# Fewer filling matmuls, range tests moved to the end, more word buffers and a new hand-written order in a fused linear-attention and gated-MLP kernel

## Chip, cores and metric

One core of a Trainium2 chip runs the whole program. The metric is the device time of one execution in microseconds (us), given as the median of some runs. A profile is one more execution, taken by the hardware profiler. Engines are named as the profile names them: PE (TensorE), DVE (VectorE), ACT (ScalarE), POOL (GpSimd), SP (SyncE, here a DMA queue).

## What is computed

The reference is a complex linear recurrence for 4 x 8 heads over 768 steps with 48 x 48 states, followed by a two-layer MLP over all 3072 tokens. In short:

```
a = (a_re + i a_im) * min(|a|, 0.999) / (|a| + 1e-6)      # per head, step, channel d
S_t = a_t * S_(t-1) + k_t v_t^T        # complex state, the real part is read
y_t = q_t . Re(S_t)
h = x @ w_in;  g = h * tanh(softplus(h));  out = g @ w_out   # 384 -> 2048 -> 384
```

## The kernel before

**Tiling.** The 3072 tokens are 12 *units* of 256 tokens (4 batches, 3 units each); a unit is two *chunks* a and b of 128. For each unit `elementwise` (L319) turns a_re and a_im into growth factors and phases: squares, logarithms, exponentials, arctan, sine and cosine on ACT, products, scans and roundings on DVE; q and k are multiplied by them and sent through DMAs ("relays", L534) into the row layout `T`. Units 0 and 1 (`SUMMED`) take their running sums by matmuls against triangular constants `turn` and `less` (`sum_up`, L381) in place of DVE scans. `attention` (L556) does a chunk as matmuls: transposes of k (`kn`), the causal 128 x 128 products (`am`), the output (`y`), the state (`pd`, `hold`). DMAs (`x move`, L675) lay y out as the MLP's input `x`. `moe` (L698) then runs 8 column blocks: first product `mm1` (L720), gate chain exp, cap, square, ln, inv on ACT and DVE, `gate` (L733), second product `mm2` (L757). Unit 0 is "plain": fp32 operands (192 first-product and 64 second-product matmuls, half a unit at a time, blocks `q0` to `q3` for halves a and b). Units 1 to 11 use three fp32r products of high and low parts (`xH`, `xL`, `wh`, `wl`; blocks `p0` to `p7`).

**Weights.** `weight(i)` (L256) loads one of 16 weight tiles as 64-bit words in a two-buffer pool (`words`, L263) and rebuilds it bit by bit: `low` (ACT or DVE), `shift`, `join` (DVE, L274, L278), `carry` (POOL or DVE, L282). `halves(i)` (L290) later makes `wh` (`high`, L298) and `wl` (`rest`, L303).

**Order.** Every step is registered as an operation with a list of engines allowed; the literal `ORDER` (L52) gives the sequence in which all operations are issued and, by a letter, an engine other than the first allowed one. Each engine executes its own operations in that sequence and waits where one is not ready; so do the DMA queues of SP and ACT. A position below is the index in that sequence. Buffers are taken in the same sequence.

**Filling.** 69 `spin` operations (L816, `SPINS`, L41) of two bf16 matmuls of 512 columns each, "junk", stand between PE's other operations from the start up to the second products of unit 0's half b; their PSUM tile has the tag `po`, two buffers, which the second products use too (L814).

**Range test.** For all units a `test` (L456) on DVE counts the elements with a_re - 0.55 >= a quarter of a_im squared into `good`; at the end `verdict` (L820) sums these counts, and a general path runs if one fails.

Of the kernel before, what the change touches and what calls it, by code (L numbers as in the profile page):

```python
# [55 lines left out]
146 202 149 231 72 148 71 206 204 108 234 236 151 150 68 154 237 73 207 200 156 208 600 152 240 109 157 465 155 181
160 238 601 175 161 203 239 182 209 602 183 176 177 184 178 110 153 245 185 179 241 393 217 394 180 467 111 242 218
187 186 389 219 243 189 220 188 244 192 205 392 190 390 463 193 391 191 250 195 246 196 221 247 305 222A 396 223 224A
599 194 400 398 469 306 399 248 401A 402 210 197 307 249 397 604 403 316 213 212 211 255 471 308 408A 608 409 606 309
315 407 251 777 252 310 419 214 317 253 112 325 311 318 420 254 312 256 113 215 319 313 609 320 260 114 611 610 115  # L60
216 421 257 321 423 605 473 314 258 422 404 424 425 259V 430 261 262 427 265 411 405 336 475 426 413 406 263 414 412A
428 415 607 264 431 322 417A 416 616 433 429 776 434 418 266 335 784 267 270 617 477 326 268 781 432 116 269 612 117
327 436 118 119 120 782 275 345 479 328 613 121 329 122 271 123 124 337 272 125 615 435 273 126 614 127 338 128 274
276 277 129 130 339 131 783 132 133 340 134 280 627A 437 481V 135 341 278 136 330 438 440 618 395 619 279 331 137 332
323 342 439V 324 281 282 285 483 410 283 442 598 626A 620 597 346 284 441 443 356 621 347 485 290 355 286 348 287 333
623 628 288 357 464 334 622 289 358 447 450 343 624 966 349 295 625 365 291 359 344 350 292 629 448 360 445 293 351
630 444 361 635 352 294 296 362 632 451 446 636 634 353 487 453 489 454 354 456 455 297 363 637 449 298 639 364 461
457V 638 452 299 459 462 300 375 631 640 780 491 366 458 642 460 466 965 376 641 367 786 633 301 368 496 302 369 468
643 377 495 370 303 644 645 470 371 304 647 646 372 788 649 778 378 779 507 497 508 648 650 651 785 379 652 970 472
380 373 787 973 474 381 374 789 498 382 499 654 476 385 520 509 655 386 478 500 383 790 510 480 501 656 791 792 519  # L70
482 653 493 657 384 484 511 971 793 659 512 658 661 387 502 513 388 660 521 532 662 972 522 663 503A 514 523 794 664
515A 524 531 969 665 504 796 667 516 544 533 668 797 795 505 666 534 525 798 669 806 807G 506 535 672 536 543 526 670
808G 537 673 517 674 799 545 555 675 538 527 556 800 528 518 557 546 539 547 558 529 540 548 801 559 530 549 486 560
541 550 803 542 488 492 567 804 810 568 551A 805 579 552 569 813 817 811 553 816 580 561 814 570 671 818 571 562 554
820 572 494 676 822 581 563 573 812 582 677 564 583 819 574 584 815 565 490 575A 823 585 802 689 821 576 678 1157 586
# [967 lines left out]
```

## Time and profile before

| | |
|---|---|
| median of 3 runs | 615.82 us (615.81 to 618.37) |
| the profiled execution | 614.4 us |
| its span, first to last instruction | 612.7 us |
| PE, DVE, ACT busy | 596.7, 465.5, 496.8 us |
| instructions | 12061 |

The profiled execution is 1.7 us longer than its span and 1.4 us shorter than the median. Busy time is the union of an engine's instructions; a busy PE includes the junk.

### The profile page before, as it was taken

How to read it: one execution, taken by the hardware profiler on the slowest of the kernel's cores; microseconds unless marked ns; L12 is line 12 of the kernel's file. 1: busy time of each engine (PE TensorE's matmuls, PEld its weight loads, DVE VectorE, ACT ScalarE, POOL GpSimd, SP SyncE). 2: the span in 40 equal slices, each digit the busy share in tenths (PEclk: the TensorE clock that was granted, in tenths of full speed). 3: DMA queues.
4: the chain of work that ended last, by engine and by line, in shares of the span. 5: the costliest groups of instructions: out<-in, count | busy, mean ns of one | idle time of the engine just before them, and what ended most of it. 6: DMA issues, size and time to landing. Idle time of an engine off the chain costs nothing.

```text
span 612.7 us, 12061 instructions
## 1 busy us (share of the span) xinstructions
PE 596.7 (97%) x4712; PEld 555.4 (91%) x4712; DVE 465.5 (76%) x806; ACT 496.8 (81%) x790; POOL 48.8 (8%) x45
## 2 busy tenths in 40 slices
PE   8999999899999999999999999999999999999995
PEld 4688777889899999999999999999999999999995
DVE  5999788899889979996969969848967455455352
ACT  8899877798899999999989999868995615659381
POOL 1122343101000110000000001000011000000000
PEclk9999999999999999999999999999999999999999
DMA  8777765711516354135234153115144030020000
GB/s 287 225 231 212 233 197 166 207 54 28 173 57 169 92 154 132 43 103 168 79 116 118 53 152 89 46 50 133 53 130 105 22 84 1 2 53 2 28 1 30
DMA packets 56673, 65.51 MB, mean 107 GB/s; under 512 B 4768, under 2 KB 50208, under 8 KB 56608
## 3 DMA queue, kind: packets, MB, share of 16 engines
q1 hardware_dynamic: 55952, 64.16, 36.1%
q8 instruction: 39, 0.64, 0.4%
q10 hardware_dynamic: 656, 0.49, 0.3%
q14 instruction: 26, 0.21, 0.1%
HBM read 36.18 MB, written 4.72 MB: 67 GB/s over the span
## 4 chain that ended last, share of the span: by engine, by line
PE 49%; ACT 28%; DVE 9%; DMA 5%; issue 4%; SPq 3%; POOL 0%; ACTq 0%; DVEq 0%; POOLq 0%
PE po L757 17%; PE ph L720 17%; ACT e L170 11%; ACT X L170 6%; ACT L168 5%; PE junk L818 5%; PE pa L594 4%; PE ypsum L612 3%; SPq L534 2%; PE pd L625 2%; DMA T<-X 1%; ACT R L170 1%; DVE g L733 1%; DMA x<-y 1%; DVE gl L745 1%
## 5 line engine op out<-in xcount | busy, mean ns | idle before, releaser
L720 PE MATMUL ph<-xH,wh 128*128 128x256 f32 x462 | 133.1, 288 | 1.9 <-DVE g L733 1.8
L720 PE MATMUL ph<-xL,wh 128*128 128x256 f32 x462 | 129.8, 281 | 0.0
L720 PE MATMUL ph<-xH,wl 128*128 128x256 f32 x462 | 129.7, 281 | 0.0
L170 ACT ACTIVATE e<-e 128x512 f32<-128x512 f32 x192 | 117.2, 626 | 11.2 <-DVE e L789 10.3
L757 PE MATMUL po<-wh,gh 128*128 128x384 f32 x308 | 106.4, 346 | 0.0
L757 PE MATMUL po<-wh,gl 128*128 128x384 f32 x308 | 104.4, 339 | 0.0
L757 PE MATMUL po<-wl,gh 128*128 128x384 f32 x308 | 104.1, 338 | 0.0
L720 PEld LDWEIGHTS ph<-xH,wh 128*128 128x128 f32 x462 | 87.0, 188 | 4.5 <-DVE g L733 2.3
L733 DVE SCALAR_TENSOR_TENSOR g<-e,ph 128x512 f32<-128x512 f32 x96 | 65.3, 683 | 31.4 <-ACT e L170 28.4
L720 PEld LDWEIGHTS ph<-xL,wh 128*128 128x128 f32 x462 | 87.0, 188 | 0.1
L720 PEld LDWEIGHTS ph<-xH,wl 128*128 128x128 f32 x462 | 87.0, 188 | 0.0
L168 ACT ACT_TABLE_LOAD x58 | 74.4, 1283 | 1.4 <-issue 0.4
L789 DVE TENSOR_SCALAR e<-e 128x512 f32<-128x512 f32 x96 | 46.3, 485 | 35.6 <-ACT e L170 35.0
L170 ACT ACTIVATE e<-ph 128x512 f32<-128x512 f32 x96 | 56.6, 592 | 17.4 <-PE ph L720 14.6
L745 DVE TENSOR_TENSOR gl<-g,gh 128x512 fp32r<-128x512 f32 x88 | 61.6, 703 | 10.7 <-PE po L757 7.2
L170 ACT ACTIVATE e<-e,fifth 128x512 f32<-128x512 f32 x96 | 68.5, 720 | 1.0
L757 PEld LDWEIGHTS po<-wh,gh 128*128 128x128 f32 x308 | 57.9, 188 | 0.7 <-issue 0.7
L757 PEld LDWEIGHTS po<-wh,gl 128*128 128x128 f32 x308 | 57.9, 188 | 0.3 <-DVE gl L745 0.2
L757 PEld LDWEIGHTS po<-wl,gh 128*128 128x128 f32 x308 | 57.8, 188 | 0.0
L594 PE MATMUL pa<-T 96*128 96x128 f32 x384 | 48.8, 277 | 0.6 <-DVE S L636 0.4
L594 PEld LDWEIGHTS pa<-T 96*128 96x128 f32 x384 | 46.2, 191 | 2.3 <-DVE S L636 0.6
L601 DVE TENSOR_TENSOR am<-pa,cmask 128x512 f32<-128x512 f32 x48 | 32.3, 686 | 7.7 <-PE pa L594 7.3
(128 smaller groups left out, 1094.1 us busy)
## 6 DMA issues: line engine op xcount, KB each, us to landing
T<-X SPq DMA_DIRECT2D x71, 129.0 KB, 2.5
T<-QK SPq DMA_DIRECT2D x70, 129.0 KB, 2.5
words<-w_in SPq DMA_DIRECT2D x8, 768.0 KB, 4.6
words<-w_out SPq DMA_DIRECT2D x8, 768.0 KB, 5.2
QK<-k SPq DMA_DIRECT2D x12, 384.0 KB, 4.5
QK<-q SPq DMA_DIRECT2D x12, 384.0 KB, 4.5
V<-v SPq DMA_DIRECT2D x12, 384.0 KB, 3.8
out_dram<-o SPq DMA_DIRECT2D x24, 192.0 KB, 1.9
```

The source lines that it names most:

```text
L168: self.nc.scalar.preload_act_table_set(need)
L170: return self.nc.scalar.activation(out, in_, func, **kw)
L534: e.dma_start(to[part * NJ + j], st[src][:, c, j])
L594: e.matmul(d["pa", g][:, i, :], T()[:, 4 * g + i, 1, :C], T()[:, 4 * g + i, 0, :C], start=True, stop=True)
L601: e.tensor_tensor(d["am", g], d["pa", g], cmask.unsqueeze(1).broadcast_to([P, 4, C]), ALU.mult)
L612: e.matmul(ypsum[64 * par:64 * par + D, i, :], lhs, rhs, start=m == 0, stop=first or m == 1)
L720: e.matmul(ph[k][:, slot(k, j, a), :], win(x, j, kt, a), st[y][:, kt, cols(k)], start=n == 0, stop=n + 1 == len(todo))
L733: e.scalar_tensor_tensor(g_[k], e_[k], 2.5, ph[k], ALU.subtract, ALU.mult)
L745: e.tensor_tensor(gs[k][1], g_[k], gs[k][0].bitcast(F32), ALU.subtract)
L757: e.matmul(po[t], x[:, slot(k, j, a), 0 if halved else t * P:C if halved else (t + 1) * P], wout(y, j, a), start=j == 0 and a == 0 and n == 0,
L789: op("V", f"{n} cap", lambda e, k=k: e.tensor_scalar_min(e_[k], e_[k], math.exp(20.0)))
L818: e.matmul(junk["junk"], cmask, cmask.unsqueeze(1).broadcast_to([P, 4, P]), start=True, stop=True)
```

## The change

- `SPINS` goes from 69 to 40.
- Units 0 and 1 lose their four half-unit `test` operations in `steps`; a new function `test(u)` registers, with the verdict at the end, a reload of a_re and a_im, a square (ACT or DVE) and one test for each of the two units.
- Unit 1's clamp of the log magnitude, a DVE `tensor_scalar`, becomes an ACT `Relu` with scale and bias; its magnitude sum uses `less` for both halves.
- Word tiles rotate over six places: the two buffers as before, and four that later hold `wh` pairs (`wp6` to `wp3`).
- The constants are built in another sequence on POOL (`cmask` first, `identity` late); `good` is zeroed.
- `ORDER` is a new list (2434 operations, before 2459). It also chooses other engines for some: up to unit 1's first MLP product, 11 of the carries go to DVE and 3 to POOL (before 2 and 13), 3 of the `low` to DVE (before none), 13 relays and 3 x moves to the ACT queue (before 3 and 2), and 6 `high` come ahead of it on ACT (before 14). Table loads on ACT, which follow from the sequence of functions, are 44 (before 58), 12 of them ahead of that product (before 10).

```
@@ -38,8 +38,10 @@
 SPLIT_UNITS = 2
 PLAIN = (8, 0)
 HALVED = (0,)
-SPINS, SPIN = 69, 2
+SPINS, SPIN = 40, 2
+WORDS = ("words", "words", "wp6", "wp5", "wp4", "wp3")
 SUMMED = 2
+CLIPPED = (1,)
 HELD = 2
 XRUNS = ((0, 0, 0, 32), (0, 1, 32, 16), (64, 1, 64, 16), (0, 2, 80, 32))
 LOW, HIGH, FADED = 0.55, 2e6, 1e-17
@@ -49,103 +51,103 @@
 TABLE = {AF.Exp: EXPLN, AF.Ln: EXPLN, AF.Arctan: TRIG, AF.Sin: TRIG}
 
 ORDER = [(int(x.rstrip("VAGTS")), x.lstrip("0123456789")) for x in """
-74 0 1 75 2 5 76 3 77 159 7 158 78 8 4 10 79 225 9 11 230 25 80 12 6 15 13 162 26 81 595 16 82 596 27 83 18 17 28V 84
-14 30 85 29 19 31 32 20 166 21 38 23 24 86 22 41 87 163 42 88 33 47 89 164 90 43 49 34 48 91 227 165 92 167 35 93 168
...
+72 0 1 73 127 2 74 3 75 128 4 7V 76 8 5 10V 9 77 192 11G 12 197 78 79 24V 13 132V 14 19 27V 80 22 81 82 25 83 15 28 84
+133 17 85 16 135V 31 18 26 32 29 134 86 23 33 87 34 21 166V 88 20 89 42 46 47G 137 35 48 169V 136 30 90 43V 138 45 36
...
@@ -219,9 +221,22 @@
     nc.scalar.preload_act_table_set(EXPLN)
     op.table = EXPLN
 
-    identity = const.tile([P, P], F32, name="identity")
-    make_identity(nc, identity)
-    ident = identity[:2 * D, :2 * D]
+    cmask = const.tile([P, P], BF16, name="cmask")
+    nc.gpsimd.memset(cmask, 1.0)
+    nc.gpsimd.affine_select(
+        out=cmask, in_=cmask, compare_op=ALU.is_ge, fill=0.0, base=0,
+        pattern=[[1, P]], channel_multiplier=-1,
+    )
+    halfpi = const.tile([P, 1], F32, name="halfpi")
+    nc.gpsimd.memset(halfpi, math.pi / 2)
+    tiny = const.tile([P, 1], F32, name="tiny")
+    nc.gpsimd.memset(tiny, 1e-30)
+    fifth = const.tile([P, 1], F32, name="fifth")
+    nc.gpsimd.memset(fifth, 0.2)
+    clip = const.tile([P, 1], F32, name="clip")
+    nc.gpsimd.memset(clip, math.log(0.999))
+    above = const.tile([P, 1], F32, name="above")
+    nc.gpsimd.memset(above, 1.0 / 0.999)
     sums = {}
     for n, x in (("turn", INV2PI), ("less", -2.0 * INV2PI)):
         sums[n] = const.tile([P, P], F32, name=n)
@@ -230,28 +245,20 @@
             out=sums[n], in_=sums[n], compare_op=ALU.is_ge, fill=0.0, base=0,
             pattern=[[1, P]], channel_multiplier=-1,
         )
-    cmask = const.tile([P, P], BF16, name="cmask")
-    nc.gpsimd.memset(cmask, 1.0)
-    nc.gpsimd.affine_select(
-        out=cmask, in_=cmask, compare_op=ALU.is_ge, fill=0.0, base=0,
-        pattern=[[1, P]], channel_multiplier=-1,
-    )
+    identity = const.tile([P, P], F32, name="identity")
+    make_identity(nc, identity)
+    ident = identity[:2 * D, :2 * D]
     rmask = const.tile([P, NJ * NCH, C], U8, name="rmask")
     nc.gpsimd.memset(rmask, 1.0)
     nc.gpsimd.memset(rmask[:, :, 0:1], 0.0)
-    halfpi = const.tile([P, 1], F32, name="halfpi")
-    nc.gpsimd.memset(halfpi, math.pi / 2)
-    tiny = const.tile([P, 1], F32, name="tiny")
-    nc.gpsimd.memset(tiny, 1e-30)
-    fifth = const.tile([P, 1], F32, name="fifth")
-    nc.gpsimd.memset(fifth, 0.2)
     good = const.tile([P, UNITS + SPLIT_UNITS, 3], F32, name="good")
+    nc.gpsimd.memset(good, 0.0)
     ncar = const.tile([P, NJ], F32, name="ncar")
     ypsum = ps.tile([112, 4, C], F32, name="ypsum", bufs=1)
     nc.vector.memset(ypsum[32:64], 0.0)
 
 
-    w, wh, wl, words = {}, {}, {}, {}
+    w, wh, wl, words, pairs = {}, {}, {}, {}, {}
 
     def weight(i):
         src = (w_in, w_out)[i % 2][i // 2]
@@ -260,7 +267,9 @@
             return words[i].bitcast(U32).rearrange("p (n two) -> p n two", two=2)[:, :, n]
 
         def load(e):
-            words[i] = me.tile([P, WC], I64, tag="words", name="words", bufs=2)
+            slot = WORDS[i % len(WORDS)]
+            pool, bufs = (me, 2) if slot == "words" else (wts, 1)
+            words[i] = pool.tile([P, WC], I64, tag=slot, name="words", bufs=bufs)
             e.dma_start(words[i], src)
 
         def low(e):
@@ -290,7 +299,9 @@
     def halves(i):
         def high(e):
             if i < NW - 2:
-                wh[i] = wts.tile([P, WC], F32R, tag=f"w{NW + i}", name="wh")
+                if i // 2 not in pairs:
+                    pairs[i // 2] = wts.tile([P, 2, WC], F32R, tag=f"wp{i // 2}", name="wh")
+                wh[i] = pairs[i // 2][:, i % 2]
                 wl[i] = None
             else:
                 both = me.tile([P, 2, WC], F32R, tag="words", name="whl", bufs=2)
@@ -389,7 +400,7 @@
             def mag(e):
                 pm[0] = bank("mag")
                 for j in range(NJ):
-                    for a, x in enumerate(("turn", "less")):
+                    for a, x in enumerate(("less" if u in CLIPPED else "turn", "less")):
                         e.matmul(pm[0][:, j, :], st["X"][:, c, j, a, :C], sums[x], start=a == 0, stop=a == 1)
 
             def phase(e):
@@ -453,16 +464,23 @@
                 op("AV", f"{n} size i", size_i)
                 op("VG", f"{n} size", lambda e: e.tensor_tensor(half(0), half(0), half(1), ALU.add))
                 op("VG", f"{n} slope", lambda e: e.tensor_tensor(I(), I(), x1(), ALU.mult))
-                op("V", f"{n} test", lambda e: e.scalar_tensor_tensor(
-                    half(1), R(), LOW, half(1), ALU.subtract, ALU.is_ge, accum_out=good[:, gi(g), 0:1]))
+                if not summed:
+                    op("V", f"{n} test", lambda e: e.scalar_tensor_tensor(
+                        half(1), R(), LOW, half(1), ALU.subtract, ALU.is_ge, accum_out=good[:, gi(g), 0:1]))
                 op("A", f"{n} arctan", lambda e: act(I(), I(), AF.Arctan))
                 op("A", f"{n} mag ln", lambda e: act(half(0), half(0), AF.Ln, scale=4.0, bias=tiny))
                 op("A", f"{n} mag exp", lambda e: act(half(1), half(0), AF.Exp, scale=-0.5))
-                op("A", f"{n} mag eps", lambda e: act(half(1), half(1), AF.Ln, scale=1e-6, bias=1.0))
-                op("V", f"{n} mag clamp", lambda e: e.tensor_scalar(
-                    half(0), half(0), 2.0 * math.log(0.999), -1.2, ALU.min, ALU.max))
+                if u in CLIPPED:
+                    op("A", f"{n} mag eps", lambda e: act(half(1), half(1), AF.Ln, scale=1e-6 / 0.999, bias=above))
+                    op("A", f"{n} mag clip", lambda e: act(half(0), half(0), AF.Relu, scale=-0.5, bias=clip))
+                else:
+                    op("A", f"{n} mag eps", lambda e: act(half(1), half(1), AF.Ln, scale=1e-6, bias=1.0))
+                    op("V", f"{n} mag clamp", lambda e: e.tensor_scalar(
+                        half(0), half(0), 2.0 * math.log(0.999), -1.2, ALU.min, ALU.max))
                 if summed:
-                    sum_up(n, g)
+                    for c in (g,) if isinstance(g, int) else range(NCH):
+                        sum_up(n if isinstance(g, int) else f"{n}{'ab'[c]}", c)
+                        yield
                     return
                 op("V", f"{n} mag", lambda e: e.scalar_tensor_tensor(R(), half(0), 0.5, half(1), ALU.mult, ALU.subtract))
                 op("V", f"{n} mag scan", lambda e: e.tensor_tensor_scan(
@@ -545,11 +563,19 @@
 
         for late in (False, True):
             for g in groups:
-                steps(g, late)
-                if summed and not late:
-                    yield
+                yield from steps(g, late)
         if not summed:
             yield
+
+    def test(u):
+
+        st = Tiles({"R": (io, "R", 2, [P, NJ * TU]), "I": (io, "I", 2, [P, NJ * TU])})
+        op("S", f"R{u} again", lambda e: e.dma_start(st["R"], are[u]))
+        op("S", f"I{u} again", lambda e: e.dma_start(st["I"], aim[u]))
+        op("AV", f"u{u} size again", lambda e: act(st["I"], st["I"], AF.Square, scale=0.5) if e is nc.scalar
+           else e.scalar_tensor_tensor(st["I"], st["I"], 0.25, st["I"], ALU.mult, ALU.mult))
+        op("V", f"u{u} test", lambda e: e.scalar_tensor_tensor(
+            st["I"], st["R"], LOW, st["I"], ALU.subtract, ALU.is_ge, accum_out=good[:, u, 0:1]))
 
     state = {}
 
@@ -855,6 +881,8 @@
             for i in range(NW):
                 halves(i)
         if u + 1 == UNITS:
+            for i in range(SUMMED):
+                test(i)
             verdict()
         moe(u, units[u], u * TU)
     with tc.manual_schedule():
```

## Rows read from the trace of the kernel before

**Rows 1.** The page: busy time by engine (us, share of the span, instructions), and its group of DVE's cap (busy us, mean ns of one, idle before).

```profile
PE 596.7 (97%) x4712; PEld 555.4 (91%) x4712; DVE 465.5 (76%) x806; ACT 496.8 (81%) x790; POOL 48.8 (8%) x45
...
L789 DVE TENSOR_SCALAR e<-e 128x512 f32<-128x512 f32 x96 | 46.3, 485 | 35.6 <-ACT e L170 35.0
```

**Rows 2.** Busy time in stretches of the span: from:to, length, then busy us and instruction count of PE, PEld, DVE, ACT, POOL, the granted clock as a share of full speed, DMA share, GB/s.

```profile
0.00:83.00 83.00, 78.79 (x574) 57.20 (x574) 65.97 (x112) 74.11 (x127) 22.46 (x27) 1.00 0.73 228
83.00:110.30 27.30, 27.25 (x184) 21.65 (x185) 24.99 (x36) 18.65 (x28) 8.92 (x5) 1.00 0.69 202
110.30:200.00 89.70, 86.20 (x694) 81.24 (x693) 81.18 (x134) 82.09 (x129) 4.38 (x3) 1.00 0.40 112
200.00:300.00 100.00, 99.08 (x807) 95.74 (x805) 87.98 (x151) 99.44 (x153) 3.77 (x4) 1.00 0.38 108
300.00:600.00 300.00, 298.88 (x2426) 293.43 (x2425) 204.00 (x373) 220.93 (x353) 9.26 (x7) 1.00 0.24 66
```

**Rows 3.** The chain of waits that ended last, followed back from the end: start us, length us, engine and line; the pieces with junk.

```profile
2.57 7.20 PE junk L818 x24
...
13.11 6.04 PE junk L818 x28
...
74.40 6.91 PE junk L818 x32
...
83.05 2.85 PE po L757 x8
```

**Rows 4.** From the timeline: weight loads of the first junk matmuls, PE's first matmul of unit 1's MLP, and DVE's gate for unit 0's half b, block q0 (start us, duration us).

```profile
2.97 0.15 PEld L818 LDWEIGHTS <-cmask 128*128 128x128 bf16 x1 [0.28 <-issue]
3.40 0.15 PEld L818 LDWEIGHTS <-cmask 128*128 128x128 bf16 x1 [0.28 <-issue]
...
6.37 2.90 PEld L818 LDWEIGHTS <-cmask 128*128 128x128 bf16 x14 [0.26 <-issue]
...
64.67 0.68 DVE L733 SCALAR_TENSOR_TENSOR g<-e,ph 128x512 f32<-128x512 f32 x1
...
110.31 0.36 PE L720 MATMUL ph<-xH,wh 128*128 128x256 f32 x1
```

**Rows 5.** DVE in the timeline (a start follows the one before it by less than a duration, since instructions overlap by some 0.09 us): the prices of carry, join, shift, squares, test, clamp.

```profile
17.57 0.57 DVE L274 TENSOR_SCALAR w<-words 128x768 uint32<-128x768 uint32 x1
18.04 0.43 DVE L462 TENSOR_SCALAR X<-X 128x384 f32<-128x384 f32 x1
...
19.24 0.56 DVE L456 SCALAR_TENSOR_TENSOR X<-R,X 128x384 f32<-128x384 f32 x1
...
20.93 0.96 DVE L282 CUSTOM_DVE_ANT_0 w<-words,w 128x1536 uint16<-128x1536 uint16 x1
21.80 0.96 DVE L447 SCALAR_TENSOR_TENSOR X<-I 128x768 f32<-128x768 f32 x1
```

**Rows 6.** POOL's carries and DVE beside them, from the timeline.

```profile
23.61 0.96 DVE L503 TENSOR_TENSOR QK<-QK,X 128x768 f32<-128x768 f32 x1
...
28.58 2.09 DVE L456 SCALAR_TENSOR_TENSOR X<-R,X 128x384 f32<-128x384 f32 x1
...
34.19 2.07 DVE L462 TENSOR_SCALAR X<-X 128x384 f32<-128x384 f32 x1
...
40.06 1.85 POOL L282 TENSOR_TENSOR w<-w,words 128x768 int32<-128x768 int32 x1 [4.08 <-DVE w L278]
...
40.44 2.29 DVE L503 TENSOR_TENSOR QK<-QK,X 128x768 f32<-128x768 f32 x1
```

**Rows 7.** DVE's and ACT's costliest groups in the first 110 us: busy us, mean ns.

```profile
L789 DVE TENSOR_SCALAR e<-e 128x512 f32<-128x512 f32 x7 | 7.0, 999 | 5.2 <-ACT e L170 5.2
...
L479 DVE SCALAR_TENSOR_TENSOR I<-ncar,I 128x3 f32<-128x3 f32 x1 | 1.2, 1224 | 0.0
...
L170 ACT ACTIVATE words<-words 128x768 int32<-128x768 uint32 x15 | 13.8, 923 | 0.9 <-DMA words<-w_out 0.8 <-DMA words<-w_in 0.2
L168 ACT ACT_TABLE_LOAD x10 | 12.8, 1283 | 0.5 <-issue 0.4
L298 ACT CAST wh<-w 128x768 fp32r<-128x768 f32 x13 | 10.6, 824 | 0.9 <-ACT words L170 0.7 <-POOL w L282 0.2
```

**Rows 8.** The ACT queue's DMA issue, and waits of ACT and DVE for a weight tile, from the timeline (in brackets the idle time before and what ended it); last, from the view of DMA issues, the loads of a_re (KB each, median us to landing).

```profile
45.23 0.63 ACTq L534 DMA_DIRECT2D T<-QK  x1
45.90 1.28 ACT L168 ACT_TABLE_LOAD   x1 [0.37 <-issue]
...
112.36 0.56 DVE L274 TENSOR_SCALAR w<-words 128x768 uint32<-128x768 uint32 x1 [2.05 <-DMA words<-w_out]
...
112.36 0.93 ACT L170 ACTIVATE words<-words 128x768 int32<-128x768 uint32 x1 [2.50 <-DMA words<-w_out]
...
R<-a_re SPq DMA_DIRECT2D x10, 384.0 KB, 3.8
```

**Rows 9.** Stretches of 20 us as in rows 2, and the end.

```profile
20.00:40.00 20.00, 19.15 (x155) 14.26 (x155) 18.16 (x33) 17.91 (x34) 3.90 (x2) 1.00 0.82 240
40.00:60.00 20.00, 19.53 (x167) 16.78 (x162) 18.52 (x26) 18.41 (x31) 6.42 (x3) 1.00 0.72 216
...
520.00:540.00 20.00, 20.00 (x146) 19.75 (x146) 9.87 (x18) 10.62 (x19) 0.00 (x0) 1.00 0.00 1
...
609.00:612.70 3.70, 0.00 (x0) 0.00 (x0) 0.00 (x0) 0.49 (x1) 0.00 (x0) 0.70 0.15 55
```

More of the change, by code (lines that the diff above doesn't have):

```diff
@@ L56 @@
[L56 to L75, printed above, removed]
[7 rows of a table removed]
@@ new lines @@
+1558 1556 1250 1718 1251 1270 1559V 1721 1288 1557 1719 1260 1271 1289 1722 1261 1724 1560 1886 1290 1562 1720 1881
+1262 1887 1272 1279 1561V 1394 1280 1273 1281 1291 1263 1725 1292 1282 1274 1293 1283 1730 1393 1294 1284A 2055 1275
+1727 1285 1395 1729 1295 1564 1731 1563 1296A 2054 1405 1882 1552 1723 1396 1286 1297 1565 1287 1406 1298 1407 1397
+1408 1299 1883 1398 1409 1418 1300 1302 1717 1417 1399 1303 1410 1301 1400 1567 1688 1885 1419 1566 2062 1420 1569
+1401 1411 1402 1568 1571 1888 1421 1430 1574 1422 1412 1728 1572 1423 1429 1576 1424 1441 1726 1431 1577 1432 1442
@@ new lines @@
+1488 1598 1599 1608 1489 1906 1600 1609 1590 2069 1743 1908 1491 1490 1741 1744 1909 1591 1740 1492 1610 1900 1601
+1745 2246 1907 1602 1748 1746 1901 1611 1603 1750 1612 1747 1613 1620 1742V 1904 1614 1592 1911 1621 1749 1902 1593
+1632 1903 1751 1622 1604A 1615 2245 1633 1910 2071 1905 1594 1623 1634 1605 1752 2076 1635 1753 1636 1913 1624 1754V
+1915 1625 1595 2077 2072 1758 1626 1755 1637 1645 1757 2250V 1606 1912 2253V 2251 1627 1756 1644 2074 1616 2058 1628
+1638 1617 1656 1646 1763V 2056 1764 2252 1647 1607 2057 1639 1648 2073 1657 1629 1649 1759V 1618 2078 1650 1761 1669
@@ new lines @@
+1793 1935 1936 1803 1794 1804 1937 1785 1795 1774 1805 1941 1940 1786 1806 2103 1938V 1775 1807 1796 1945 2262 1813
+1947 1797 2101 1814 1942 1808 1946 2263 1776 1944 1815 2095 1825 2100 2271 2327 1787 2094 2088 1943 1948 1950V 1788
+1798 1816 2247 1951 1826 1952V 2248 1949 1953 1837 2326 2104V 1827 1809 1817 2105 1810 2265 2107 2106 1799 1818 2108
+2272 2109 2114 2110 2111 2264 1828 2115 2112 2116 1819 2275 1829 2119 1838 2277A 1830 1820 1800 2276 2120V 1839 2117
+1849 1831 1821 2118G 1840 2273 1850 2274 2121 1832 2123 1822 1811 1833A 1851 1812 1954 1841 1852 2279 1842 1823 1843
@@ new lines @@
+2018 1999 2009 2019 2293 2295 2020 1988 2021 1989 2144 2294 2039 2027 2000 2028 2010A 2297 2038 2298 2029 2145 2296V
+2040 2329 2030 2001 2031 2032 2146 2332 2033 2299 2041 2147 2304 2300 2301 2148 2011 2149 2302 2022 2305 2034 2306
+2303 2042 2309 2307 2333 2043 2311 2150 2044 2158 2045 2157 2023 2308 2012 2310 2159 2151 2013 2024 2035 2046A 2025
+2036 2047 2312 2037 2048 2049 2313 2050 2052 2152 2051 2314 2334 2053 2160 2153 2169 2161 2154 2170 2182 2171 2162
+2172 2181 2163 2173 2155 2164 2174 2194 2315 2175 2316 2183 2156 2176 2319 2184 2318 2193 2165 2185 2166 2317 2186
@@ new lines @@
+2205 2177 2320V 2187 2206 2324 2188 2195 2322V 2196 2167 2207 2208 2335 2217 2178 2209 2189 2197 2168 2198 2218 2199
+2210 2200 2179 2211 2323 2190 2219 2180 2212 2220 2191 2321 2221 2222 2192 2201A 2213 2336 2223 2229 2224 2230 2325
+2202 2338 2214 2231 2232 2337 2233 2203 2339 2234 2204 2235 2215 2236 2225 2350 2226 2340 2349 2341 2216 2351 2237A
+2352 2227 2342 2238 2353 2228 2354 2343 2239 2355 2240 2361 2241V 2243V 2242 2362 2344 2244 2345A 2373 2363 2346 2374
+2364 2356 2365 2347 2366 2375 2385 2367 2376 2357 2377 2386 2358 2368 2348 2387 2378 2359 2388 2369 2379 2397 2389
@@ L149 @@
+2380 2370 2398 2409 2399 2390 2360 2391 2371 2392 2400 2410 2401 2402 2421 2381A 2393 2411 2382 2372 2412 2383 2413
+2394 2403 2422 2404 2405 2384 2423 2414 2395 2406 2415 2424 2396 2416 2425 2417 2426 2407 2418 2427 2408 2428 2419
+2429A 2430 2420 2431 2432 2433A
 """.split()]
```

116 lines of the change are left out of this document (64 added, 52 removed), and 26 rows, old and new, of the table ORDER.

## The prediction, made before the changed kernel ran

> **What bounds the kernel now.** Read first where each engine is busy, then the same by stretches, then who waits. Over the whole span TensorE (PE) is busy 596.7 of 612.7 us [rows 1], but that holds the junk. By stretches [rows 2], from 110.3 to 600 us PE stands still for 3.5 + 0.9 + 1.1 = 5.5 us: there it is the bound, and nothing on the other engines pays. Before 83 us it stands still for only 4.2 us too, of which 2.6 before its first instruction, yet this is no real load: the chain shows pieces of junk as long as 7.2, 6.0 and 6.9 us [rows 3]. A warm junk matmul takes 6.91 / 32 = 0.216 us there; the first ones load their weights 0.43 us apart [rows 4]. So 138 of them cost 9 x 0.43 + 129 x 0.216 = 31.7 us of PE's order.
>
> What does real work wait for in this front? ACT is busy 74.1 and DVE 66.0 of 83 us [rows 2]: the two together feed PE, ACT somewhat more. I take as mark M the first matmul of unit 1's MLP, at 110.3 us [rows 4]. What PE has to do before and after M is the same in both orders within one or two blocks. So the question is when M comes; the 502.4 us behind it stay, as PE is the bound there. Up to M real work takes 110.3 - 2.6 (start) - 31.7 (junk) - 1.7 (other waits) = 74.3 us.
>
> **The change, part by part.**
>
> *Fewer spins.* 58 matmuls x 0.216 = 12.5 us leave PE's order. All lie ahead of M. PE's floor for M becomes 110.3 - 12.5 - 1.7 = 96.1 us. It is reached only if operands come that early. One point speaks for it: the gate for half b's first block is done at 64.67 + 0.68 = 65.4 us, but its second product starts at 83.05, behind the last piece of junk [rows 3, 4]; junk holds one of the two `po` buffers until then. In the new order the last spin stands ahead of half b's first product, so the buffer is free long before.
>
> *DVE up to M.* It is busy 66.0 + 25.0 = 91.0 us there [rows 2]. Counted from both orders, with prices start to start [rows 5]: nine more carries x 0.87 = 7.8; three `low`, not seen on DVE before (as `shift`, which reads the same words with the same stride, 0.47; as the carry at most 0.87, which adds 1.2; I take the first) = 1.4; seven half squares x 0.47 and a full one of 0.87 = 4.2; two weight subtractions x 0.87 = 1.7; three evictions = 1.5. That is 16.6 more. Gone: four tests x 0.56 = 2.2, two clamps 0.9, roundings 1.4, a size and a slope 0.9, one join 0.9, a cast and copies 0.7: 7.0. Net +9.6.
>
> *POOL's carries.* Against this stands what a carry on POOL does to DVE. With one running, a product takes 2.29 us instead of 0.96, a test 2.09 instead of 0.56, a clamp 2.07 instead of 0.43 [rows 5, 6]; the seven caps have a mean of 0.999 against 0.485 over the kernel [rows 1, 7]; a link of three elements takes 1.22 [rows 7]. Excess: 1.3 + 1.5 + 1.6 + 3.6 + 1.1 = 9.1 us for 13 carries, 0.7 each; ten fewer give back 7.0. Two half-width operations of units 0 and 1 go to POOL instead: +0.7 by half that price each. The ends are 0 and 9.1. DVE's busy time to M becomes 91.0 + 9.6 - 7.0 + 0.7 = 94.3 us. The Trainium skill (SBUF — State Buffer, "Who interferes with whom") has the loser of the port that DVE and GpSimd share blocked for the whole instruction of the other; by that, ten carries of 1.85 us would give back up to 18.5 us, DVE would fall to 85.8 us, and M to PE's floor. The rows show only 9.1 in all, as many carries fall beside work that needs no second port or wait themselves; I keep 7.0.
>
> *ACT up to M.* Busy 74.1 + 18.7 = 92.8 us [rows 2]. Off: four `low` (0.92 each) 3.7, eight `high` (0.82) 6.6 [rows 7], squares and their readings about 4; on: two more table loads 2.6 [rows 7], clips, roundings and more of the gate chain about 4. It comes to about 85. Eleven more DMA issues go through ACT's queue: one takes 0.63 and left ACT idle for 0.37 [rows 8], so 0 to 6.9 us, at 0.37 each 4.1. ACT ends at 89, under DVE: the bound in front passes from ACT to DVE. What waits behind those issues is ACT's own next activation, and a relay there also waits for DVE's turn product; this belongs to the use of the engines below.
>
> *Word buffers.* The wait for a weight tile just behind M, 2.05 us on DVE and 2.50 on ACT [rows 8], comes from a two-buffer pool; with six places the loads go out earlier. It lets DVE keep its pace up to M; I book nothing apart.
>
> *When M comes.* Between 20 and 60 us DVE was busy 36.7 of 40 us, a share of 0.917 [rows 9], the best long stretch of the front that is not held by PE. I take this share: 94.3 / 0.917 = 102.8 us, 7.5 earlier than 110.3. Between M and PE's floor 6.7 us of waits then stand where junk stood. The ends: the floor of 96.1, and DVE's share over the whole front before, 91.0 / 110.3 = 0.825, which gives 114.3.
>
> *Behind M.* Eight `high` come after M now (6.6 us of ACT); ACT had 7.6 us free up to 200 us and none up to 300 [rows 2], but 16 table loads fewer behind M give it 20.5 us. DVE has 8.5 and 12 free there against some 10 us more work spread to the end. I book nothing; without that cover up to 2 us.
>
> *Tests at the end.* Two squares and two tests of 0.96 us each and four loads of 3.8 us [rows 5, 8], placed where DVE is busy 9.9 of 20 us and DMA idle [rows 9]. SP's queue takes the reloads between unit 11's relays; the third waits for unit 11's last reading of R. Nothing booked; up to 1 us if relays come late. The other start sequence on POOL lets junk begin up to 1 us earlier; nothing, as later waits take it up.
>
> **Sum.** Span 612.7 - 7.5 = 605.2. The profiled execution lies 1.7 us above its span and the median 1.4 above that (615.82 against 614.4): 605.2 + 3.1 = 608.3 us.
>
> **Rivals.**
>
> *The floor.* Junk was pure delay and M comes at 96 to 97: 615.8 - 14.2 = 601.6 us. For it: the second product that stood 17.7 us behind its gate. Against: DVE would need 0.98 of its time.
>
> *Waits take the place of all the junk.* M stays at 110: 616 us, no change. For it: DVE and ACT have together almost the same work, 183.8 before and 183 after, and both were near 0.9 in the first 60 us. Against: ACT was idle for a third of 83 to 110 us [rows 2], so the front as a whole has room.
>
> *Slower: DVE, now the busiest, is used no better than before.* At 0.825 M comes at 114.3, 4 us late: 619.8. It decides where DVE's share to M is under 0.83. For it: in-order waits on ACT, whose queue now holds relays.
>
> *Slower: the clock.* The granted clock is 1.00 in all stretches up to the end, 0.70 in the last 3.7 us, when PE had nothing left to do [rows 2, 9]. At the start junk comes every 0.43 us against 0.216 later, the spacing of 1.2 against 2.4 GHz [rows 3, 4]. Behind the last spin PE has no filler, with up to 17 us of waits to M if DVE is slow. If the clock falls to 1.2 GHz for matmuls worth 10 us, they take 20, half of it hidden in waits: 114.3 + 5, 625 us. The Trainium skill (TensorE: Matmul & The Clock Gate, Part 1) calls the throttled rate the default, which activity releases; by that rule filling less costs. The end of the trace agrees, no wait inside it does (none is that long).
>
> *The new places don't bring the weights sooner,* since loads queue on SP behind relays: the 2 us at M stay, 610.3 us.
>
> **How the numbers follow.** Forecast (M from 98 to 106, 603.5 to 611.5): 0.55. Floor 0.10. Weights late 0.05. No change 0.16. DVE slower 0.08. Clock 0.06. A measurement here tells about 0.5%, 3.1 us, from no change. Faster by more than that: 0.55 + 0.10 + 0.05 = 0.70; same 0.16; slower 0.14. The range 601 to 617 takes in the floor and the case of no change, and leaves out the two slow ones, 0.14.
>
> **What would show it.** Right: 80 junk matmuls, the last before 65 us; M near 103; DVE's busy time to M 92 to 97 us at a share near 0.92, ACT's under it; single carries on DVE of 0.96; PE idle some 5 to 9 us between 20 us and M, on DVE or relays; granted clock 1.00 up to M; the 500 us behind M as before. Wrong: M at 110 or later, idle time of PE behind M well over 6 us, a clock under 1.00 in the front, or PE waiting for unit 11's relays near the reloads.

## The result and the profile of the changed kernel

The changed kernel takes 600.87 us (median of 4 runs, 598.65 to 603.12) against 615.82 for the kernel before (4 runs, 615.72 to 618.37): ratio 0.9748, 95% interval 0.97 to 0.9795. It is faster, as forecast, but by 14.95 us instead of 7.5, and 0.1 us below the lower end of the range. The profiled execution took 601.94 us, its span 600.2. That execution lies 1.1 us above its median, the profiled one of the kernel before 1.4 under its own; so the spans, which the traces explain, differ by 12.5 us and not by 14.95.

The sum of the prediction can be laid beside the trace at two places, the mark M (PE's first matmul of unit 1's MLP) and the last matmul. First the timeline at M, then the last matmul (start us, duration us):

```profile
107.93 0.58 PE L746 MATMUL ph<-xH,wh 128*128 128x256 f32 x1
...
594.36 0.34 PE L783 MATMUL po<-whl,gh 128*128 128x384 f32 x1
```

| us | before | after | forecast | measured |
|---|---|---|---|---|
| start to M | 110.3 | 107.9 | -7.5 | -2.4 |
| M to the end of the last matmul | 496.2 | 486.8 | 0 | -9.4 |
| behind it | 6.2 | 5.5 | 0 | -0.7 |
| span | 612.7 | 600.2 | -7.5 | -12.5 |

So the total came nearer than its parts by luck: the front gave a third of its forecast, the stretch that was booked at nothing gave most of the gain, and the two errors partly cancel. The 9.4 us are firm: in eight further kernels that keep the changed order behind M (runs 2 to 6 and 10 to 12 below) that stretch takes 486.8 to 487.3 us, and 495.9 in the old order of run 1. The 2.4 us are less so: M came at 110.3, 112.4 (run 7) and 112.1 (run 8) in three profiles of the same old front, and at 107.9 and 107.5 (run 9) in two of the new one.

The stretches, to be laid beside [rows 2] (columns as there):

```profile
0.00:83.00 83.00, 71.95 (x520) 56.55 (x521) 65.62 (x123) 60.91 (x101) 10.76 (x26) 0.94 0.73 241
83.00:107.90 24.90, 24.90 (x181) 20.45 (x181) 24.30 (x34) 24.64 (x40) 2.45 (x1) 1.00 0.43 139
107.90:200.00 92.10, 91.66 (x747) 87.68 (x746) 89.20 (x155) 90.77 (x140) 8.84 (x5) 1.00 0.46 133
200.00:300.00 100.00, 100.00 (x837) 98.39 (x836) 89.51 (x158) 85.75 (x136) 1.60 (x1) 1.00 0.36 99
300.00:594.00 294.00, 294.00 (x2373) 290.40 (x2372) 203.47 (x378) 206.32 (x333) 5.23 (x4) 1.00 0.25 71
```

See first that in [rows 2] PE is busy 99.08 of 100 us from 200 to 300, here 100.00, a difference of 0.9 us; but it ran 807 matmuls there and runs 837 here. From M to 300 us it ran 694 + 807 = 1501 in 189.7 us, 126.4 ns each, and now 747 + 837 = 1584 in 192.1, 121.3 ns each. Behind 300 us it is 300 / 2426 = 123.7 and 294 / 2373 = 123.9 ns, the same. So most of the 9.4 us lie between M and 300 us (1501 x 5.1 ns = 7.7, if the mix of matmuls is alike). Now the whole stretch from M to the last matmul, first before, then after, with 3957 and 3956 matmuls:

```profile
110.30:606.50 496.20, 490.65 (x3957) 476.58 (x3955) 374.55 (x659) 403.57 (x635) 17.41 (x14) 1.00 0.29 82
107.90:594.70 486.80, 486.36 (x3956) 476.86 (x3954) 382.18 (x689) 383.02 (x607) 15.67 (x10) 1.00 0.32 89
```

PE's idle time falls from 5.55 us to 0.44, which is 5.1 of the 9.4. The other 4.3 us lie in its busy time, 490.65 against 486.36 for the same work at the same granted clock. They are most likely short waits that the trace counts as busy, since ends of matmuls are modelled; no row shows them one by one.

Then all waits of PE, which is the whole list (us in total, times, longest):

```profile
PE pkn L608 <- DMA T<-QK: 5.8, 2, 5.2
PE pkn L608 <- DMA R<-a_re: 3.4, 1, 3.4
PE junk L844 <- POOL cmask L226: 1.7, 1, 1.7
PE pa L620 <- ACT kn L613: 0.3, 1, 0.3
PE psum L409 <- ACT I L172: 0.2, 1, 0.2
```

All but the 0.3 lie before M. For the second, the trace names the load of `a_re` as what came last; the matmul reads `T`, and a relay to `T`, issued on ACT's queue at 20.96 us, landed 5.8 us later, just before the wait ended. The chain of waits says the same by engine, first the kernel before, then the changed one:

```profile
PE 49%; ACT 28%; DVE 9%; DMA 5%; issue 4%; SPq 3%; POOL 0%; ACTq 0%; DVEq 0%; POOLq 0%
```

```profile
PE 78%; ACT 10%; DMA 5%; DVE 3%; issue 2%; SPq 1%; POOL 0%; DVEq 0%; ACTq 0%; POOLq 0%
```

In the front, the stretches that answer to [rows 9], and from the timeline the two waits with what stands around the second (in brackets the idle time before and what ended it):

```profile
20.00:40.00 20.00, 16.64 (x127) 13.43 (x125) 16.96 (x33) 11.94 (x21) 6.53 (x3) 0.91 0.80 243
40.00:60.00 20.00, 19.39 (x184) 18.16 (x182) 20.00 (x33) 17.64 (x31) 0.28 (x1) 1.00 0.73 245
60.00:80.00 20.00, 14.84 (x110) 12.40 (x109) 12.29 (x25) 11.26 (x19) 0.00 (x0) 0.83 0.85 296
```

```profile
27.05 0.87 PE L608 MATMUL pkn<-identity,T 96*128 96x96 f32 x4 [3.37 <-DMA R<-a_re]
...
66.06 1.46 PE L783 MATMUL po<-w,g 128*128 128x384 f32 x4
...
72.68 1.51 PE L608 MATMUL pkn<-identity,T 96*128 96x96 f32 x8 [5.16 <-DMA T<-QK]
73.98 2.82 PE L783 MATMUL po<-w,g 128*128 128x384 f32 x4
```

The same four matmuls take 1.46 us before the wait of 5.16 and 2.82 behind it: TensorE runs there at the lower of its two clocks, 1.2 in place of 2.4 GHz. The granted clock is 0.50 from 72.7 to 76.5 us, and 0.83 over the stretch. Of the table of M: PE starts 0.9 us earlier, junk takes 9 x 0.43 + 71 x 0.216 = 19.2 us instead of 31.7 (the last piece starts at 51.2), other waits take 11.1 - 1.7 = 9.4 instead of 1.7, and the rest 77.6 instead of 74.3 for as many matmuls (621 and 620): -0.9 - 12.5 + 7.7 + 3.3 = -2.4. The 3.3 more are, by estimate, work at the low clock: behind the two waits PE is busy for some 8.7 us at 0.50, which can cost up to 4.4.

What PE waited for at 72.68 is a relay. The DMA issues of that time:

```profile
61.69 0.53 SPq L370 DMA_DIRECT2D R<-a_re  x1
62.32 0.46 SPq L273 DMA_DIRECT2D words<-w_in  x1
62.83 0.45 SPq L273 DMA_DIRECT2D words<-w_out  x1
63.33 0.42 SPq L273 DMA_DIRECT2D words<-w_in  x1
63.73 0.55 ACTq L552 DMA_DIRECT2D T<-QK  x1
64.62 0.33 SPq L273 DMA_DIRECT2D words<-w_out  x1
```

Within 3 us SP's queue issues a_re (384 KB) and four weight tiles of 768 KB, a burst that the six places allow. The relay of 129 KB that ACT's queue issues among them, at 63.73, lands 8.7 us later. It is the burst and not ACT's queue: a relay that the same queue issued at 61.40, ahead of the burst, landed in 2.8 us, and the same relay in run 4 below, where one load of 768 KB is issued in place of four, in 4.2.

### The profile page after: what moved, and what is told of

Its sections match the earlier page's. It is cut to its first block, busy times and chain, and to the rows that moved or that the text cites. A ratio compares the mean times of both kernels' runs of the same rounds, so it can differ in the third digit from the quotient of the medians.

```text
span 600.2 us, 11935 instructions
## 1 busy us (share of the span) xinstructions
PE 583.2 (97%) x4654; PEld 553.9 (92%) x4654; DVE 472.1 (79%) x844; ACT 469.1 (78%) x747; POOL 28.9 (5%) x37
## 4 chain that ended last, share of the span: by engine, by line
PE 78%; ACT 10%; DMA 5%; DVE 3%; issue 2%; SPq 1%; POOL 0%; DVEq 0%; ACTq 0%; POOLq 0%
PE po L783 30%; PE ph L746 30%; PE pa L620 6%; PE ypsum L638 6%; PE pd L651 4%; ACT e L172 3%; ACT X L172 3%; DMA T<-QK 2%; PE pkn L608 2%; ACT L170 1%; DMA R<-a_re 1%; DMA QK<-k 1%; DMA V<-v 1%; ACT wh L309 1%; ACT gh L765 0%
## 5 line engine op out<-in xcount | busy, mean ns | idle before, releaser
L771 DVE TENSOR_TENSOR gl<-g,gh 128x512 fp32r<-128x512 f32 x88 | 60.9, 694 | 13.6 <-ACT gh L765 7.5
L815 DVE TENSOR_SCALAR e<-e 128x512 f32<-128x512 f32 x96 | 40.3, 421 | 32.0 <-ACT e L172 31.5
L620 PE MATMUL pa<-T 96*128 96x128 f32 x384 | 50.1, 280 | 0.3 <-ACT kn L613 0.3
L620 PEld LDWEIGHTS pa<-T 96*128 96x128 f32 x384 | 47.5, 195 | 1.6 <-ACT kn L613 0.5
L627 DVE TENSOR_TENSOR am<-pa,cmask 128x512 f32<-128x512 f32 x48 | 32.5, 685 | 13.6 <-PE pa L620 13.6
```

The lines of the kernel that those rows point to most:

```text
L620: e.matmul(d["pa", g][:, i, :], T()[:, 4 * g + i, 1, :C], T()[:, 4 * g + i, 0, :C], start=True, stop=True)
L627: e.tensor_tensor(d["am", g], d["pa", g], cmask.unsqueeze(1).broadcast_to([P, 4, C]), ALU.mult)
L771: e.tensor_tensor(gs[k][1], g_[k], gs[k][0].bitcast(F32), ALU.subtract)
L815: op("V", f"{n} cap", lambda e, k=k: e.tensor_scalar_min(e_[k], e_[k], math.exp(20.0)))
```

## The experiments

All ratios are against the kernel before, run on the same chip as the run: medians 616.28 us (runs 1, 4, 5, 8), 615.53 (2, 3, 6, 7) and 615.84 (9 to 12), single executions 613.8 to 620.1. M and what stands behind it come from one profiled execution of each. "Behind M" is the time from M to the end of the last matmul.

**1. The old order with 40 spins.**

```
+    spun = []
     def spin(e):
-        for _ in range(SPIN):
+        spun.append(0)
+        for _ in range(SPIN if len(spun) <= 40 else 0):
```

> The kernel before with its last 29 spins empty (40 left, 80 junk matmuls), its order untouched. T1 (junk was delay): the mark M, PE's first matmul of unit 1's MLP, comes 4 to 9 us earlier than 110.3 and the time is 607 to 612. T2 (waits take the junk's place, DVE and ACT bound the front): M stays within 2 us and the time is 614 to 618. T3 (clock): the granted clock falls under 0.95 in the stretch of 60 to 85 us and the time is over 618.

616.56 us, ratio 1.001 (0.9981 to 1.0039); M at 110.81. Waits stand where junk stood, on ACT (4.53 us), relays and DVE, and the clock falls behind them:

```profile
60.00:80.00 20.00, 12.76 (x111) 11.38 (x109) 14.52 (x22) 16.72 (x26) 7.64 (x3) 0.85 0.56 179
80.00:100.00 20.00, 18.96 (x118) 15.33 (x120) 17.19 (x27) 15.80 (x24) 8.14 (x4) 0.89 0.67 223
```

Up to M PE stands still for 13.6 us, 9.3 more than before, and its work without junk takes 78.0 us instead of 74.3. So of the 12.5 us of junk some 9 only filled time, and some 3.7 went, by estimate, to matmuls at the low clock. Fewer spins alone are worth nothing.

**2. The new order with 138 junk matmuls.** The last eight spins have 9 or 10 matmuls instead of 2.

```
+        for _ in range(SPIN if len(spun) <= 32 else 9 if len(spun) <= 38 else 10):
```

> The changed kernel with its last eight spins longer, so that 138 junk matmuls run as before (58 more, 12.5 us, between 36 and 52 us). T1 (junk there is delay, but waits near 55 and 73 us take up to 6 us of it): M comes 5 to 12 us later than 107.9, the time 605 to 612. T2 (waits take up all of it): M within 2 us, the time 599 to 602.

609.54 us, ratio 0.9905 (0.9876 to 0.9935); M at 116.38, 8.5 us later for 12.5 us of junk, behind M 486.8 as in the changed kernel. In the new order two thirds of this junk is delay. Together with run 1: leaving out spins pays only in the order as changed. That holds for junk at these places, from 37 to 60 us; the old one went on to 83.

**3. The ten carries back on POOL.**

```
+POOLED = (211, 216, 221, 231, 236, 241, 246, 256, 261, 266)
+ORDER = [(i, "" if i in POOLED else e) for i, e in ORDER]
```

> The changed kernel with ten carries back on POOL. T1 (prediction: DVE saves 8.7 us and loses about 7 to the shared use): M within 2 us of 107.9, time 599 to 603. T2 (a carry on POOL holds DVE and comes later itself): DVE's operations stretch as before, M at 110 to 114, the time 603 to 608.

605.88 us, ratio 0.9832 (0.9797 to 0.9867); M at 112.81, 4.9 us later. The stretch up to M (columns as before), to be held against the sum of the changed kernel's first two stretches above:

```profile
0.00:112.80 112.80, 99.85 (x700) 79.16 (x701) 93.86 (x148) 85.74 (x140) 38.82 (x36) 0.94 0.64 212
```

DVE has 148 instructions up to M instead of 123 + 34 = 157, nine carries fewer (one of the ten lies behind), yet it is busy 93.9 instead of 89.9 us. Nine carries would have taken 9 x 0.87 = 7.8, so those on POOL cost DVE 3.9 + 7.8 = 11.7 us, 1.3 each. Most of it falls on two steps of the rebuilding, shift and join; their rows up to M in this run, in the changed kernel and in the kernel before:

```profile
L285 DVE TENSOR_SCALAR w<-words 128x768 uint32<-128x768 uint32 x15 | 13.5, 901 | 0.0
L289 DVE SCALAR_TENSOR_TENSOR w<-words,w 128x768 uint32<-128x768 uint32 x14 | 16.3, 1167 | 0.1
...
L283 DVE TENSOR_SCALAR w<-words 128x768 uint32<-128x768 uint32 x15 | 8.3, 553 | 0.0
L287 DVE SCALAR_TENSOR_TENSOR w<-words,w 128x768 uint32<-128x768 uint32 x14 | 13.3, 951 | 0.0
...
L274 DVE TENSOR_SCALAR w<-words 128x768 uint32<-128x768 uint32 x15 | 8.3, 551 | 0.0
L278 DVE SCALAR_TENSOR_TENSOR w<-words,w 128x768 uint32<-128x768 uint32 x15 | 14.3, 950 | 0.0
```

In the kernel before, with 13 carries on POOL, neither was held up. So 1.3 us is the price in the new order, where the carries run beside them, and not that of the old one.

**4. Two word buffers in place of six places.**

```
-WORDS = ("words", "words", "wp6", "wp5", "wp4", "wp3")
+WORDS = ("words",)
```

> The changed kernel with all word tiles in the two-buffer pool. T1 (the four further places bring the weights sooner): DVE and ACT wait for weight tiles, M comes later than 107.9 and the time is 603 to 608. T2 (their gain is small and their burst of loads delays the relays): the 5.2 us wait near 73 us shrinks and the time is 595 to 600.

599.22 us, ratio 0.9749 (0.9711 to 0.9787); M at 104.66. The wait of 5.2 us is gone, others of 2.3 and 2.4 us have come. The granted clock from 60 to 80 us is 1.00. The places bring nothing in the order as changed.

**5. The relays ahead of the loads.** Four relays of units 0 and 1 go from ACT's queue to SP's, to where they stand ahead of the burst.

```
+for op, behind in ((384, 385), (383, 384), (51, 55), (56, 51)):
+    move(op, behind)
```

> The changed kernel with the two relays of unit 0's half a and the two of unit 1's half b that stood on the ACT queue moved to SP's queue ahead of the loads there. T1 (the burst of loads made those relays land late): PE's waits of 3.4 us near 27 and 5.2 us near 73 fall under 1 us each, M comes at 97 to 102, the clock stays at 1.00 and the time is 591 to 596. T2 (DVE or ACT are the next bound there): the waits move to another operand and the time is 598 to 602.

593.87 us, ratio 0.9664 (0.9626 to 0.9701), faster than both kernels: its slowest execution, 597.29, is under the changed kernel's fastest, 598.65. M comes at 101.44, behind M 486.8 again. The front's stretches and the largest waits of PE:

```profile
20.00:40.00 20.00, 15.19 (x119) 11.78 (x117) 16.36 (x31) 13.81 (x23) 6.32 (x3) 0.96 0.73 222
40.00:60.00 20.00, 19.84 (x178) 18.42 (x178) 19.23 (x31) 14.49 (x28) 0.00 (x0) 0.95 0.78 265
60.00:80.00 20.00, 20.00 (x161) 17.06 (x161) 19.74 (x35) 19.16 (x32) 0.00 (x0) 1.00 0.89 311
80.00:101.40 21.40, 21.40 (x158) 17.50 (x157) 21.04 (x30) 21.18 (x35) 2.44 (x1) 1.00 0.48 160
```

```profile
PE pkn L617 <- DMA words<-w_out: 2.6, 1, 2.6
PE junk L853 <- POOL cmask L235: 1.7, 1, 1.7
PE pd L660 <- DVE am L636: 1.4, 1, 1.4
```

The waits of 3.4 and 5.2 us are gone, while SP still issues the same burst, now behind the relays; from 60 us to M PE stands still no more, and DVE is busy 19.74 + 21.04 of 41.4 us. Four positions in a list were worth 6.5 us at M; the relays' order and their queue change together here.

**6. Junk in the wait.** The last two spins, with 12 matmuls each, go to where the changed kernel waits 5.2 us.

```
+for op in (110, 111):
+    move(op, 280)
...
+        for _ in range(SPIN if len(spun) <= 38 else 12):
```

> The changed kernel with its last two spins moved to the wait ahead of unit 1's half b (near 67 us) and lengthened to 12 matmuls each, 5.2 us of junk. T1 (the fall of the clock costs matmul time): the granted clock stays at 1.00 from 60 to 80 us, the matmuls behind 73 us run at full rate, M comes 2 to 4 us earlier, the time is 596 to 599. T2 (the half rate is hidden behind other waits): M within 1 us, the time 600 to 602.

601.43 us, ratio 0.977 (0.9702 to 0.9839); M at 110.01, later and not earlier. The clock is 1.00 from 60 to 80 us, as the first theory had it, but 0.67 from 20 to 40, behind the other wait, where it was 0.91 in the changed kernel. How much of the low clock follows a given wait differs from run to run; what filling is worth stays unclear.

**7. The old front with the new tail.** The first 517 operations stand as before, all others in the new sequence, with its engines and so its table loads.

```
-457V 638 452 299 ...      (from position 517 on)
+...                       (the same operations in the changed kernel's sequence)
```

> The kernel before, its order untouched up to the mark M (517 operations), and behind it all remaining operations in the sequence and on the engines of the changed kernel's order. T1 (the 9.4 us gained behind M come from the order there): M stays at 110.3, the stretch from M to the last matmul is 486 to 488 as in the changed kernel (496 before), the time 605 to 608. T2 (they come from what the new front leaves ready): that stretch stays at 494 to 497, the time 614 to 617.

610.4 us, ratio 0.9911 (0.9879 to 0.9944); M at 112.36, so the front is no better. Behind M 492.8 us, which lies between the two theories, with one wait of 4.15 at the joint of the two sequences and clock 0.96 behind it up to 200 us; from 200 to 605 us PE stands still for 0.00:

```profile
112.30:200.00 87.70, 83.55 (x669) 79.77 (x668) 79.40 (x136) 77.76 (x120) 9.71 (x5) 0.96 0.38 105
200.00:300.00 100.00, 100.00 (x832) 98.72 (x832) 90.07 (x158) 88.68 (x139) 1.59 (x1) 1.00 0.38 104
```

Measured, the new tail gives 3.4 us. Without the wait at the joint it would be some 488.6 by estimate, and 486.4 without the 2.3 us more that PE is busy than in the changed kernel (488.65 against 486.36), at a clock of 0.76 from 116 to 130 us. So the tail, with sequence, engines and table loads together, can carry all of the 9.4; how much each of the three brings is not shown here.

**8. The old order without table loads in units 3 to 11.** Their arctan, sine and cosine become squares, so their phases are left out.

```
-act(I(), I(), AF.Arctan)
+act(I(), I(), AF.Arctan if u < 3 else AF.Square)      (sine and cosine likewise)
```

> The kernel before with Square in place of arctan and sine in units 3 to 11 (phases left out there, same tiles and counts), so that no table load is left behind M; the front is untouched. T1 (behind M PE waited for ACT, in visible and hidden pieces): M stays at 110.3 and the stretch behind it falls from 502.4 to 490 to 494, the time to 603 to 608. T2 (PE is the bound behind M and other waits don't matter, as the prediction had it): 615 to 617.

611.99 us, ratio 0.9925 (0.9895 to 0.9954); behind M 493.7, 2.5 less, in the range of the first theory; the time is in neither, as M came at 112.06. From 200 to 300 us ACT is busy 80.16 us instead of 99.44 [rows 2], and still PE has waits:

```profile
200.00:300.00 100.00, 99.59 (x818) 97.07 (x818) 88.45 (x152) 80.16 (x140) 3.67 (x4) 1.00 0.39 109
```

A lighter ACT in the same sequence gives only a quarter of the 9.4.

**9. The new order with 16 more table loads,** two ahead of an exponential in each of units 3 to 10.

```
-op("A", f"{n} grow q", lambda e: act(half(0), R(), AF.Exp))
+def grow_q(e):
+    for x in (TRIG, op.table) if 3 <= u <= 10 else ():
+        nc.scalar.preload_act_table_set(x)
+    act(half(0), R(), AF.Exp)
+op("A", f"{n} grow q", grow_q)
```

> The changed kernel with 16 table loads of ACT put back (two more ahead of the exponential of `grow q` in units 3 to 10), all behind unit 1's first MLP product, 16 x 1.28 = 20.5 us of ACT. Theory 1 (behind that mark PE alone is the bound in the new order, ACT has room there): the stretch from the mark to the last matmul stays at 487 us, time within 2 us of the changed kernel's, 600 to 603. Theory 2 (the fewer loads are what made the stretch shorter): it goes back towards 496 us and the time to 606 to 610.

625.95 us, ratio 1.0132 (1.0075 to 1.0188): 25 us slower than the changed kernel, more than the loads' own 20.5. Theory 1 falls, and theory 2 expected far less. M is unmoved (107.48), behind M it is 511.5 instead of 486.8. The added loads on ACT and one wait of PE that follows, from the timeline:

```profile
125.61 2.57 ACT L490 ACT_TABLE_LOAD   x2
...
133.63 0.59 ACT L647 COPY y<-ypsum 112x512 f32<-112x512 f32 x1
```

```profile
134.36 0.43 PE L642 MATMUL ypsum<-T,S 96*48 96x128 f32 x4 [2.81 <-ACT y L647]
```

ACT's 2.57 us turn up on its way to `y`, which starts 26.15 us behind M here and 23.44 in the changed kernel, and then as 2.81 us of PE. Some of the second products behind that wait take 0.52 us instead of 0.34, at a granted clock of 0.70 from 134.3 to 140 us. Over the whole stretch behind M:

```profile
107.50:619.00 511.50, 496.34 (x3956) 483.33 (x3954) 382.40 (x689) 405.06 (x623) 15.62 (x10) 0.98 0.29 84
```

PE stands still for 15.2 us instead of 0.4 and is busy for 10.0 us more with the same matmuls, at a clock of 0.98 in place of 1.00: waits and low clock together make the 24.7 us. ACT is busy 405.1 us from there to the end, as in the kernel before (403.6) and 22 more than in the changed one (383.0), but only 79% of its time: a busy share under 1 is no room when PE follows ACT closely and PE can't catch up.

**10. Relays first, two word buffers** (runs 4 and 5 together).

> The changed kernel with the four relays ahead of the loads, and two word buffers in place of six places. Theory 1 (the six places do harm only through the burst of loads in front of relays): with the relays ahead, two buffers make loads wait for their rebuilding again and the mark comes 1 to 4 us later than with six places (101.4), time 595 to 598. Theory 2 (the places are worth nothing either way): 594 within 1 us.

597.52 us, ratio 0.9683 (0.9647 to 0.9719); M at 104.91, 3.5 later than in run 5. With the relays out of the way the six places are worth some 3.5 us at M; the executions of the two runs overlap (595.94 to 598.54 and 593.06 to 597.29).

**11. Relays first, 30 spins.**

```
+        for _ in range(SPIN if len(spun) <= 30 else 0):
```

> The changed kernel with the four relays ahead of the loads, and the last 10 of 40 spins empty, 20 matmuls or 4.3 us of PE's order less. Theory 1 (DVE, busy 0.95 to 1.00 from 40 us to the mark there, now sets the mark): mark within 1 us of 101.4, time within 1.5 us of 593.9, idle time of PE grows by about 4 us. Theory 2 (junk is still delay): mark at 97 to 98, time 590.

592.61 us, ratio 0.9623 (0.9567 to 0.9679), the fastest, though not told apart from run 5; M at 99.84, 1.6 us earlier for 4.3 us of junk. Mostly theory 1, not all of it.

**12. Relays first, 20 spins.**

> As the one before, with the last 20 spins empty, 8.6 us less. Theory 1 (DVE sets the mark): still 101 to 102, and the clock may fall where the waits now stand (0.7 to 0.9 in a stretch of 20 us), which costs up to 3 us: 593 to 597. Theory 2 (junk is delay): mark at 93 to 95, 586 to 588.

593.62 us, ratio 0.9629 (0.9597 to 0.9662); M at 100.01. DVE is the bound here from 40 us on, as its column shows, and the clock pays for a wait of 5.9 us on a relay:

```profile
20.00:40.00 20.00, 15.51 (x99) 14.92 (x100) 16.66 (x32) 11.93 (x21) 5.30 (x3) 0.66 0.69 218
40.00:60.00 20.00, 18.52 (x179) 17.64 (x179) 20.00 (x32) 17.82 (x31) 0.00 (x0) 1.00 0.84 272
60.00:80.00 20.00, 20.00 (x155) 16.70 (x155) 19.80 (x35) 19.12 (x32) 0.00 (x0) 1.00 0.93 329
80.00:100.00 20.00, 20.00 (x150) 16.33 (x149) 19.83 (x29) 19.85 (x32) 2.45 (x1) 1.00 0.46 152
```

## Where the prediction was right and where it failed

**Behind M: the step that failed.** "the 502.4 us behind it stay, as PE is the bound there", and "I book nothing". PE's busy share of 0.99 was read as proof. Two rows spoke against it and were at hand: ACT busy 99.44 of 100 us in the same stretch, and ACT with 28% of the chain. The count of matmuls gave a hint too: 126 ns each up to 300 us against 124 behind. The new tail gave 9.4 us: 5.1 of idle time, of which the prediction itself had read 5.5 and called it nothing, and 4.3 hidden in busy time. Run 7 shows that the tail brings this behind the old front too, but for a wait at the joint, run 8 that lighter ACT work alone brings 2.5, run 9 that the new sequence can't carry 16 more loads at the places where they were put. So the 20.5 us of loads that the prediction counted as mere cover may well be a condition of the gain. That is not shown: the price of the old loads at their old places stays open, and how the 9.4 divides between sequence and loads.

**Word buffers and relays on ACT's queue: the term that was missed.** The places were booked at nothing, the eleven issues at 4.1 us of ACT's idle time. What they did was to let 3.4 MB of loads go out around a relay that PE needed, and PE waited 5.2 us. Run 5 prices the order of relays and loads: 6.5 us at M. The transfer that becomes possible earlier collides with one that others wait for; the prediction asked only what the relays cost the engine that issues them.

**M by DVE's share: the step of the front that failed.** The prediction took 94.3 us of DVE's work at a share of 0.917. In the changed kernel DVE did 89.9 us at 89.9 / 107.9 = 0.833, nearly the 0.825 of the rival "DVE is used no better than before", since it too stood still around PE's wait for the late relay (busy 12.29 of 20 us from 60 to 80). Run 5 shows what held it: with the relays first M came at 101.4, near the forecast of 102.8, at 89.7 / 101.4 = 0.885. That nearness is in part luck, as both factors were too high. The share was near 0.99 behind 40 us (run 12) and 0.75 before, where the pipeline fills. The work was 4.4 us less than forecast, and only part of that is traced: carries on POOL had cost DVE more in the kernel before than the 9.1 us counted. The seven caps fell to 0.422 us each from 0.999 [rows 7], not to 0.485; and two operations beside carries weren't counted, a cast of `xH` (1.5 us instead of 0.3) and a subtraction for the phase (1.4 instead of 1.0). With these it is some 11 us, 0.9 for each carry, 1.6 us more for ten.

```profile
L815 DVE TENSOR_SCALAR e<-e 128x512 f32<-128x512 f32 x7 | 3.0, 422 | 7.5 <-ACT e L172 7.5
```

The Trainium skill (SBUF — State Buffer, "Who interferes with whom") has whichever of DVE and GpSimd comes second to their shared port pair blocked for all of the other's instruction; nine carries of 2.67 us on POOL in run 3 would be up to 24 us by that. The trace shows 11.7, half, so not all of a carry's time held DVE up.

**ACT's work up to M: right.** 85 us were forecast, 60.91 + 24.64 = 85.6 measured.

**Fewer spins: right in size, wrong as a cause.** 12.5 us left PE's order, but 7.7 us of waits and some 3.3 of slower work took their place. Run 1 shows that in the old order leaving them out buys nothing, run 2 that in the new one they cost 8.5.

**The clock: the rival's mechanism, not its price.** "Granted clock 1.00 up to M" was wrong: 0.91 and 0.83 in two stretches, behind waits of 3.4 and 5.2 us. It cost some 3.3 us by estimate, where the rival had 5 on top of a late DVE. The prediction read the first junk matmuls, 0.43 us apart, as work at the low clock; the granted clock reads 1.00 there, so the rows don't show it. The Trainium skill (TensorE: Matmul & The Clock Gate, Part 1) has the low rate as the default that activity releases; the trace now agrees inside the run, at 73.98 us, behind 5.16 us without work.

**Tests at the end: right.** They cost nothing that shows: PE has no wait behind M longer than 0.3 us.

**The rivals.** That waits take the place of junk came true for 7.7 of 12.5 us in the front. "The floor" gave 601.6, close to the time measured, but its reason did not hold: M came at 107.9, not at 96. That the places bring nothing (610.3) was right of the places (run 4), not of the time.

## What to carry to other kernels

A PE that is busy 99% can still lose some per cent to waits, here 2% behind M, of which half did not show as idle time: lay the number of matmuls per stretch beside the busy share, and look for a second engine near 100% in the same stretch. When a change gives loads more buffers, list what else goes through the DMA engines at the moment they become free to start, above all small transfers on another queue for which an engine waits. And an in-order chain that is tuned to be tight may have no room on an engine at 79%: in run 9 the 20.5 us put there came out at the end in full, and more.
